# Another order of weight slots at the turn to the second token half, earlier x sums there, and Relu on ScalarE for one more Q pair of each half

## The chip, the cores and the metric

The kernel runs on one core of one Trainium2 chip. The metric is the device time of one execution in microseconds (us), given as the median of several. All executions below were in the fast state, with a mean granted clock between 0.997 and 1.000.

## The reference

A linear attention block and a SwiGLU block read the same normalised input; the second, through a silu, gates the first.

```python
def _A_ref(x, wqkv, wo):                      # 32 heads of 32
    q, k, v = split_heads(x @ wqkv)
    phi = lambda t: jnp.where(t > 0, t + 1, jnp.exp(t)) + 1e-6
    pq, pk = phi(q), phi(k)
    kv = jnp.einsum("bhsd,bhse->bhde", pk, v)
    num, den = pq @ kv, pq @ sum(pk) + 1e-6
    return merge_heads(num / den) @ wo
def _B_ref(x, w_gate, w_up, w_down):
    return (silu(x @ w_gate) * (x @ w_up)) @ w_down
xn = _layernorm(x)                            # x is 1 x 2048 x 1024
return x + _A_ref(xn, ...) * silu(_B_ref(xn, ...))
```

(Shortened: the shapes are 2048 tokens, 1024 columns and 3584 hidden columns.)

## The kernel before

The program works on two token halves, p = 0 and p = 1. In each half it goes through pairs of weight blocks: Q ("q"), gate ("g") and up ("u"), two of the attention output ("s"), and then the down projection. Every product is done with seven block products in place of eight (a Strassen-like scheme), some of them nested twice. So the tensor engine (PE) saves multiplications, and the vector engine (DVE) pays with sums: of weights, of x, and of results in PSUM.

Every operation is recorded first, and a list scheduler inside the kernel then decides the order on each engine. It orders the operations that are ready by a deadline, from which `urgent` is subtracted. What comes out is a fixed program for each engine; at run time each engine takes its instructions strictly in that order and waits on semaphores.

```python
for o in reversed(ops):
    ...
    o.dl = d - o.urgent            # earlier deadline = earlier place
```

Weights are loaded (1 MB) into places that a ring gives out in a fixed order, and their sums are made after the load has landed:

```python
def wload(src, joint, dt=BF16, rd=()):
    s = raw_ring.take()
    dma(list(rd), [s.r], ..., src, dsem("wr%d" % s.k), 1024 * KB)
    c = cmb_ring.take()
    ...
    sums({...}, [cv[:, q] for q in range(4)], [s.r], cr)
```

The evacuation of Q and K applies phi. With `relu`, max(t, 0) comes from ScalarE (ACT) and the last step is a 16-bit sum in SBUF; without, one DVE operation reads PSUM in fp32:

```python
def phi_evac(src, src_r, out_ap, out_r, kind="ps", relu=False):
    ...
    act([src_r], [e.r], ea, src, ACT.Exp, kind)
    dve([e.r], [b.r], lambda h: h.tensor_scalar(ba, ea, 1.0, EPS_PHI, ALU.min, ALU.add), 512, 2.6)
    if not relu:
        dve([src_r, b.r], [out_r], lambda h: h.scalar_tensor_tensor(
            out_ap, src, 0.0, ba, ALU.max, ALU.add), 512)
        return
    r = rl_ring.take()
    act([src_r], [r.r], r.ap(FP16), src, ACT.Relu, kind)
    tt([r.r, b.r], [out_r], out_ap, r.ap(FP16), ba, ALU.add, True)
```

At the turn to the second half, x of that half comes back from memory into the region P, its sums are made, and the slot order for the weights is set:

```python
def turn_pass():
    for q in range(4):
        dma([named("xscr", q)], [P.reg(...)], P.at(...), x_scr[q], dsem("xl%d" % q), 512 * KB)
    combos(XV[1])
    x_inner(XV[1])
    gate[0] = 1
    raw_ring.__init__([(X, 0), (W, 16 * KB), (X, 0)] + [(W, 0), (W, 8 * KB), (W, 16 * KB)] * 5, 8 * KB)
    ...
```

Of the kernel before, what the change touches and what calls it, by code (L numbers as in the profile page):

```python
# [14 lines left out]
KB = 1024  # L15
# [304 lines left out]
def build_kernel(nc, A_x, A_wqkv, A_wo, B_w_gate, B_w_up, B_w_down, out, WINDOW=6, NWARM=15, NPE=2, LEAD=12.0):  # L320
# [12 lines left out]
    with ExitStack() as es:  # L333
# [23 lines left out]
        H = Arena("H", 84 * KB)  # L357
        X = Arena("X", 28 * KB)
        P = Arena("P", 16 * KB)
        W = Arena("W", 52 * KB)  # L360
        TM = Arena("TM", 26 * KB)
# [21 lines left out]
        ps = [es.enter_context(nc.psum_tensor("ps%d" % b, [128, 512], F32)) for b in range(8)]  # L383
# [26 lines left out]
        def sem(name):  # L410
            return es.enter_context(nc.semaphore(name))
# [4 lines left out]
        def dsem(name):  # L416
            if name not in semn:
                semn[name] = sem("d_" + name)
            return semn[name]

        PL = Plan(WINDOW, LEAD)
# [6 lines left out]
        def pe_mm(reads, writes, mms):  # L428
            return PL.op("pe", reads, writes, partial(_mm_group, mms), mm_cost(mms))
# [10 lines left out]
        def act(reads, writes, o, i, func, src="ps", **kw):  # L440
            q = PL.op("act", reads, writes, lambda h: h.activation(o, i, func, **kw),  # L441
                      nel(o) / (1000.0 if "bias" in kw or not isinstance(kw.get("scale", 1.0), float) else 1200.0)
                      + (0.055 if src == "ps" else 0.095))
            if func not in (ACT.Identity, ACT.Relu):
                PL.table(q, func)
            return q

        def dve(reads, writes, fn, n, rate=0.96):
            return PL.op("dve", reads, writes, fn, n / (rate * 1000.0) + 0.07)

        def tt(reads, writes, o, a, b, op, fast=False):
            return dve(reads, writes, lambda h: h.tensor_tensor(o, a, b, op), nel(o), 1.92 if fast else 0.96)  # L452
# [65 lines left out]
        e_ring = Ring(TM, 20 * KB, 1 * KB, 2)  # L518
        q_ring = Ring(TM, 22 * KB, 1 * KB, 2)
        B_ring = Ring(TM, 24 * KB, 1 * KB, 2)  # L520
        rl_ring = Ring(TM, 18 * KB, 1 * KB, 2)
        rr_ring = Ring(TM, 20 * KB, 2 * KB, 1)
        x_ring = Ring(W, 32 * KB, 2 * KB, 4)
        xn_ring = Ring(W, 40 * KB, 2 * KB, 2)
# [30 lines left out]
        def combos(v, after=None):  # L555
            for o, a, b in (("T3", "R11", "R01"), ("T1", "R01", "R00"), ("T2", "R11", "T1"), ("T4", "R10", "T2")):
                for h in range(2):
                    w = {}
                    for nm in (o, a, b):
                        ap, r = v[nm]  # L560
                        n = len(r.keys) // 2
                        w[nm] = ap[:, 2 * h:2 * h + 2, :], Region(r.keys[n * h:n * h + n])
                    q = tt([w[a][1], w[b][1]], [w[o][1]], w[o][0], w[a][0], w[b][0], ALU.subtract, True)
                    if after is not None:
                        q.preds.add(after)
                        after.succs.append(q)
# [142 lines left out]
        def feed(pair):  # L709

            prev = last_pair[0]
            if pair is None or not pair.joint:
                if prev is not None:
                    for w in TAIL:
                        prev.do(w)
                if pair is not None:
                    for w in HEAD:
                        pair.do(w)
            else:
                for w in LINK:  # L720
                    if w[0] == "n":
                        pair.do(w[1:])
                    elif prev is not None:
                        prev.do(w)
            last_pair[0] = pair
# [116 lines left out]
            return ar.at(j * 8 * KB + k * 4 * KB, 4 * KB, FP16).rearrange("p (q t) -> p q t", t=512)[  # L842
                :, :, m * 128:(m + 1) * 128]

        def phi_evac(src, src_r, out_ap, out_r, kind="ps", relu=False):
            e = e_ring.take()
            ea = e.ap(FP16)
            act([src_r], [e.r], ea, src, ACT.Exp, kind)
            b = B_ring.take()
            ba = b.ap(FP16)  # L850
            dve([e.r], [b.r], lambda h: h.tensor_scalar(ba, ea, 1.0, EPS_PHI, ALU.min, ALU.add), 512, 2.6)  # L851
            if not relu:
                dve([src_r, b.r], [out_r], lambda h: h.scalar_tensor_tensor(  # L853
                    out_ap, src, 0.0, ba, ALU.max, ALU.add), 512)
                return
            r = rl_ring.take()
            act([src_r], [r.r], r.ap(FP16), src, ACT.Relu, kind)
            tt([r.r, b.r], [out_r], out_ap, r.ap(FP16), ba, ALU.add, True)

# [12 lines left out]
        def k_evac(i, j, ap, r, kind):  # L872
            if i not in pkv:
                pkv[i] = pk_ring.take()
            s = pkv[i].sub(j * 1024, 1024)
            phi_evac(ap, r, s.ap(), s.r, kind, True)

        def v_dest(i, j):
            return vext[i % 4][:, 4 * j:4 * j + 4, 0:128]
# [67 lines left out]
        for n, (fn, args) in enumerate(((x_load, (0,)), (x_load, (1,)), (wkv_load, (0, 1, 0)), (wkv_load, (0, 1, 1)),  # L947
# [3 lines left out]
            k = len(PL.ops)  # L951
# [6 lines left out]
        for n in range(6):  # L958
            o = pe_mm(wz_r[:1], [bank_r[kvb[2]]], [(ps[kvb[2]][:, 0:128], wz[:, 0:128], wz[:, 0:128], True, True)])
# [74 lines left out]
        for q, kb in enumerate(kvb):  # L1034
            n = 3 if q < 2 else 2
            src = ps[kb][:, 0:129 * n].rearrange("p (g n) -> p g n", n=129)[:, :, 128:129]
# [43 lines left out]
        raw_ring = Places([(W, o * KB) for o in (0, 8, 16)], 8 * KB)  # L1080
# [51 lines left out]
        def xset(stat, w, xv, evac, dring):  # L1132
            def ops(m):
                ws, wr = stat(w, m)
                xa, xr = xv[XOF[m]]
                return 4, [([(ws[q], xa[:, q, :]) for q in range(4)], [wr, xr])]
            return Set(ops, evac, dring)
# [5 lines left out]
        def x_inner(v, xin=xin, places=IN_AT):  # L1143

            for m, at in zip((1, 5), places):
                ap, r = v[XOF[m]]
                B = {(k, j): ap[:, 2 * k:2 * k + 2, 256 * j:256 * j + 256] for k in range(2) for j in range(2)}
                t = [(a.at(o, KB, FP16).rearrange("p (k t) -> p k t", t=256), a.reg(o, KB)) for a, o in at]
                tt([r], [t[1][1]], t[1][0], B[1, 1], B[0, 1], ALU.subtract, True)
                tt([r], [r], B[0, 1], B[0, 1], B[0, 0], ALU.subtract, True)  # L1150
                tt([r], [t[0][1]], t[0][0], B[1, 1], B[0, 1], ALU.subtract, True)
                tt([r, t[0][1]], [t[2][1]], t[2][0], B[1, 0], t[0][0], ALU.subtract, True)
                xin[m] = {1: (B[0, 0], r), 2: (B[1, 0], r), 3: (B[1, 1], r), 5: (B[0, 1], r), 6: t[0], 7: t[1], 4: t[2]}

        def joint_of(jstat, s0, s1, xin=xin):
            def ops(m):
                def f(k):
                    ws, wr = jstat(m, k)
                    xa, xr = xin[m][k]
                    return [(ws[q], xa[:, q, :]) for q in range(2)], [wr, xr]  # L1160
                return f
            return {"1": Joint(ops(1), lambda w, b: (s0, s1)[w].put1(b)),
                    "5": Joint(ops(5), lambda w, b: (s0, s1)[w].put5(b))}
# [20 lines left out]
        def pq_tile(g, j):  # L1184
            o = PQ0 + ((2 * (g // 4) + j) * 4 + g % 4) * KB
            return H.at(o, KB, BF16), H.reg(o, KB)

        def q_pair(p, s, stats, at, go=True):
            stat, jstat = stats

            def evac(w):
                def f(i, j, ap, r, bank):
                    g = 2 * (2 * s + w) + i
                    o, orr = pq_tile(g, j)
                    phi_evac(ap, r, o, orr, "ps" if bank is not None else "sb")
                return f
            s0, s1 = (xset(stat, w, XV[p], evac(w), d_ring) for w in range(2))
            pair = Pair(s0, s1, joint_of(jstat, s0, s1) if QJ[p][s] else None, at)
            if go:
                feed(pair)  # L1200
            return pair
# [489 lines left out]
        def turn_pass():  # L1691

            for q in range(4):
                dma([named("xscr", q)], [P.reg(q * 4 * KB, 4 * KB)], P.at(q * 4 * KB, 4 * KB, FP16), x_scr[q],
                    dsem("xl%d" % q), 512 * KB)
            combos(XV[1])
            x_inner(XV[1])
            gate[0] = 1
            raw_ring.__init__([(X, 0), (W, 16 * KB), (X, 0)] + [(W, 0), (W, 8 * KB), (W, 16 * KB)] * 5, 8 * KB)
            cmb_ring.__init__([(X, 8 * KB), (W, 28 * KB), (X, 8 * KB)] + [(W, 24 * KB), (W, 32 * KB)] * 8, 8 * KB)  # L1700
            in_ring.__init__([(W, 14 * KB), (TM, 8 * KB), (W, 24 * KB), (W, 26 * KB), (W, 42 * KB), (W, 44 * KB)]
                             + [(W, 40 * KB), (TM, 8 * KB), (W, 42 * KB), (W, 44 * KB)] * 8, 2 * KB)
            pump(1)
            last_pair[0] = q_pair(1, 0, got["q", 1, 0], {}, False)
            return last_pair[0]
# [102 lines left out]
```

## Time and profile before

| | before |
|---|---|
| device time, first three executions | 713.54 us (713.01 to 713.55) |
| span of the profile | 711.2 us |
| PE busy | 704.1 us |
| vector engine busy | 634.0 us |
| ScalarE busy | 416.6 us |
| HBM traffic | 127 GB/s over the span |

PE is busy 99% of the span, so what can be won is the time in which it stands still. That time is best measured from the start of one matmul to the start of the next: here 0.216 us for 512 columns and 0.109 us for 256. What is over that I call "lost". The prediction below shows the lines and the three places in the middle of the program where time is lost: near 130, 408 and 431 us.

### The profile page before, as it was taken

What the parts mean: (1) busy time and instruction counts of PE and PEld (TensorE: products, weight loads), DVE (VectorE), ACT (ScalarE), POOL (GpSimd) and SP (SyncE); (2) the same over time, 40 slices, a digit from 0 to 9 for tenths busy, and PEclk for the clock granted to TensorE, in tenths of its full rate; (3) what the DMA queues carried; (4) which work ended last, traced back from release to release, by engine and by line L of the source; (5) the groups of instructions that cost most, each with busy time, mean ns of one, the idle gap of its engine ahead of it and who ended that gap; (6) DMA issues with size and microseconds to landing.
All of it is one profiled execution on the core that took longest, in us unless ns stands there. A gap on an engine that the chain in (4) does not pass through costs nothing.

```text
span 711.2 us, 11395 instructions
## 1 busy us (share of the span) xinstructions
PE 704.1 (99%) x4170; PEld 388.4 (55%) x4181; DVE 634.0 (89%) x1533; ACT 416.6 (59%) x809; POOL 14.1 (2%) x35
## 2 busy tenths in 40 slices
PE   9999999999999999999999999999999999999997
PEld 4444445555555555555555455555555555565654
DVE  7999858999999999988966999999999999798863
ACT  4788755888679566664212156776886756531212
POOL 2111000000000000000000000000000000000000
PEclk9999999999999999999999999999999999999999
DMA  9654134345664252326485954132816241656663
GB/s 295 149 119 90 30 118 126 112 140 187 182 180 145 93 171 94 119 66 175 139 190 172 254 160 149 60 119 94 207 60 189 79 149 60 178 141 162 142 156 96
DMA packets 140870, 98.64 MB, mean 139 GB/s; under 512 B 34960, under 2 KB 137872, under 8 KB 140816
## 3 DMA queue, kind: packets, MB, share of 16 engines
q1 hardware_dynamic: 140528, 97.74, 49.3%
q8 instruction: 32, 0.52, 0.3%
q10 hardware_dynamic: 288, 0.20, 0.1%
q14 instruction: 22, 0.18, 0.1%
HBM read 77.59 MB, written 12.71 MB: 127 GB/s over the span
## 4 chain that ended last, share of the span: by engine, by line
PE 92%; DVE 5%; DMA 2%; issue 1%; ACT 0%; SPq 0%
PE ps L309 92%; DMA X<-in_A_wqkv_dram 1%; DVE TM L452 1%; DVE ps L452 1%; DVE W L452 1%; DVE H L853 1%; DVE X L452 0%; DMA W<-in_A_x_dram 0%; ACT TM L441 0%; DVE H L1043 0%; DVE TM L851 0%; PE ps L316 0%; DVE P L452 0%; DVE stats L773 0%; SPq L455 0%
## 5 line engine op out<-in xcount | busy, mean ns | idle before, releaser
L309 PE MATMUL ps<-X,W 128*128 128x512 f16 (+2 forms) x1372 | 288.8, 350 | 0.4 <-DVE ps L452 0.4
L441 ACT ACTIVATE TM<-ps 128x512 f16<-128x512 f32 (+3 forms) x380 | 199.6, 552 | 100.9 <-PE ps L309 97.6
L309 PE MATMUL ps<-H,W 128*128 128x512 f16 (+2 forms) x1090 | 217.9, 350 | 0.4
L452 DVE TENSOR_TENSOR W<-W 128x1024 f16<-128x1024 bf16 (+5 forms) x416 | 185.8, 479 | 5.3 <-PE ps L309 4.5
L309 PEld LDWEIGHTS ps<-X,W 128*128 128x128 f16 (+1 forms) x1372 | 132.3, 98 | 104.1 <-DVE ps L452 1.2
L309 PEld LDWEIGHTS ps<-H,W 128*128 128x128 f16 (+1 forms) x1096 | 106.1, 98 | 94.8 <-DVE ps L452 0.6
L452 DVE TENSOR_TENSOR ps<-ps,TM 128x256 f32<-128x256 f32 (+1 forms) x250 | 131.3, 527 | 13.6 <-PE ps L309 10.8
L441 ACT ACTIVATE ps<-ps 128x512 f32<-128x512 f32 (+1 forms) x174 | 85.6, 492 | 94.5 <-PE ps L309 94.0
L309 PE MATMUL ps<-P,W 128*128 128x256 f16 (+1 forms) x516 | 99.7, 319 | 0.0
L441 ACT ACTIVATE H<-ps 128x512 f16<-128x512 f32 (+1 forms) x126 | 74.7, 604 | 39.4 <-PE ps L309 39.4
L452 DVE TENSOR_TENSOR H<-H 128x1024 f16<-128x1024 f16 (+5 forms) x126 | 71.2, 578 | 0.5 <-ACT H L441 0.4
L441 ACT ACTIVATE TM<-TM 128x512 f16<-128x512 f32 (+1 forms) x68 | 42.3, 627 | 48.4 <-DVE TM L452 47.0
L309 PEld LDWEIGHTS ps<-P,W 128*128 128x128 f16 (+1 forms) x516 | 50.3, 98 | 29.0 <-ACT TM L441 0.4
L309 PE MATMUL ps<-W 128*128 128x256 f16 (+1 forms) x330 | 62.0, 282 | 1.0 <-DVE ps L452 1.0
L452 DVE TENSOR_TENSOR TM<-ps,TM 128x512 f32<-128x512 f32 (+3 forms) x63 | 41.5, 659 | 12.6 <-PE ps L309 12.1
L452 DVE TENSOR_TENSOR H<-H,TM 128x512 f16<-128x512 f16 x112 | 44.9, 416 | 7.1 <-ACT H L441 7.0
L309 PEld LDWEIGHTS ps<-W 128*128 128x128 f16 (+1 forms) x330 | 31.3, 98 | 32.9 <-DVE ps L452 2.7
L452 DVE TENSOR_TENSOR TM<-TM 128x512 bf16<-128x512 f16 (+2 forms) x73 | 29.4, 411 | 6.5 <-ACT TM L441 3.9
L309 PE MATMUL ps<-H,X 128*128 128x512 bf16 (+1 forms) x147 | 34.6, 379 | 0.2
L309 PE MATMUL ps<-H,P 128*128 128x512 bf16 (+1 forms) x108 | 26.4, 379 | 0.1
L452 DVE TENSOR_TENSOR H<-ps,TM 128x512 f16<-128x512 f32 (+1 forms) x35 | 24.0, 686 | 2.3 <-PE ps L309 1.5
L309 PEld LDWEIGHTS ps<-H,X 128*128 128x128 f16 (+1 forms) x150 | 14.3, 98 | 17.0 <-DMA H<-in_A_wqkv_dram 0.6
(95 smaller groups left out, 400.2 us busy)
## 6 DMA issues: line engine op xcount, KB each, us to landing
W<-in_B_w_gate_dram SPq DMA_DIRECT2D x14, 1024.0 KB, 5.4
W<-in_B_w_up_dram SPq DMA_DIRECT2D x13, 1024.0 KB, 5.6
W<-in_B_w_down_dram SPq DMA_DIRECT2D x14, 896.0 KB, 6.1
H<-in_A_wqkv_dram SPq DMA_DIRECT2D x8, 512.0 KB, 8.2
H<-r_scratch SPq DMA_DIRECT2D x32, 128.0 KB, 3.8
W<-m_scratch SPq DMA_DIRECT2D x4, 1024.0 KB, 5.4
s_scratch<-TM SPq DMA_DIRECT2D x32, 128.0 KB, 2.0
TM<-in_A_x_dram SPq DMA_DIRECT2D x16, 256.0 KB, 3.7
```

The source lines that it names most:

```text
L309: last = h.matmul(o, l, r, start=st, stop=sp, skip_group_check=True)
L441: q = PL.op("act", reads, writes, lambda h: h.activation(o, i, func, **kw), nel(o) / (1000.0 if "bias" in kw or not isinstance(kw.get("sca ...
L452: return dve(reads, writes, lambda h: h.tensor_tensor(o, a, b, op), nel(o), 1.92 if fast else 0.96)
L853: dve([src_r, b.r], [out_r], lambda h: h.scalar_tensor_tensor(out_ap, src, 0.0, ba, ALU.max, ALU.add), 512)
```

## The change

The intent is to take the vector engine off PE's path at those places. The first up weights of half 2 go to a free place (W 0) and not to X 0, where the first Q weights still lie (W, X and P are regions of the on-chip memory, and W 0 is the first place in W); the x sums of half 2 get an earlier deadline; and two more Q pairs let ScalarE do the Relu.

```diff
-        rl_ring = Ring(TM, 18 * KB, 1 * KB, 2)
+        rl_rings = Ring(TM, 18 * KB, 1 * KB, 2), Ring(H, 40 * KB, 1 * KB, 2)
...
-            if not relu:
+            if relu is None:
...
-            r = rl_ring.take()
+            r = relu.take()
...
-            phi_evac(ap, r, s.ap(), s.r, kind, True)
+            phi_evac(ap, r, s.ap(), s.r, kind, rl_rings[0])
...
-                    phi_evac(ap, r, o, orr, "ps" if bank is not None else "sb")
+                    phi_evac(ap, r, o, orr, "ps" if bank is not None else "sb", rl_rings[p] if s == p else None)
...
+            k = len(PL.ops)
             combos(XV[1])
             x_inner(XV[1])
+            for o in PL.ops[k:]:
+                o.urgent = 6.0
...
-            raw_ring.__init__([(X, 0), (W, 16 * KB), (X, 0)] + [(W, 0), (W, 8 * KB), (W, 16 * KB)] * 5, 8 * KB)
+            raw_ring.__init__([(X, 0), (W, 16 * KB), (W, 0), (X, 0), (W, 8 * KB), (W, 16 * KB)] + [(W, 0), (W, 8 * KB), (W, 16 * KB)] * 5, 8 * KB)
```

More of the change, by code (lines that the diff above doesn't have):

```diff
@@ L843, in xt_half, with phi_evac @@
                 :, :, m * 128:(m + 1) * 128]
-        def phi_evac(src, src_r, out_ap, out_r, kind="ps", relu=False):
+        def phi_evac(src, src_r, out_ap, out_r, kind="ps", relu=None):
             e = e_ring.take()
```

## The prediction

> **What bounds the kernel now.** I read the page's first part first, then the slices. Columns of the first line: busy time, share of the span, number of instructions. In the slices, one digit is 17.8 us.
>
> ```profile
> PE 704.1 (99%) x4170; PEld 388.4 (55%) x4181; DVE 634.0 (89%) x1533; ACT 416.6 (59%) x809; POOL 14.1 (2%) x35
> ...
> PE   9999999999999999999999999999999999999997
> ...
> DVE  7999858999999999988966999999999999798863
> ACT  4788755888679566664212156776886756531212
> PEclk9999999999999999999999999999999999999999
> ```
>
> The tensor engine is busy in every slice at full clock, and the vector engine is full in most of them. The change alters no matmul (4180 in both built programs, same shapes), so all it can win is the time in which PE stands still. That is at most 711.2 - 704.1 = 7.1 us of the span, and much of it is the start and the end, which the change does not touch. So I looked for PE's gaps one by one, in its instructions in order of time (columns: start, duration, engine, line, operation, count; in brackets the idle time before it and what ended it).
>
> ```profile
> 128.72 1.25 PE L309 MATMUL ps<-X,W 128*128 128x256 f16 x6
> 130.26 0.39 PE L309 MATMUL ps<-W 128*128 128x256 f16 x2 [0.30 <-DVE ps L452]
> ...
> 406.35 1.03 PE L309 MATMUL ps<-W 128*128 128x512 f16 x4
> 408.06 0.39 PE L309 MATMUL ps<-W 128*128 128x256 f16 x2 [0.68 <-DVE ps L452]
> ...
> 429.71 1.03 PE L309 MATMUL ps<-X,W 128*128 128x512 f16 x4
> 431.09 1.04 PE L309 MATMUL ps<-X,W 128*128 128x512 f16 x4 [0.35 <-DVE ps L452]
> ```
>
> The three gaps after the opening that name a releaser all end with a vector add from PSUM to PSUM. The bracket understates them: the end of a matmul is modelled and includes a tail. From start to start, a 512-column matmul takes 0.216 us here and a 256-column one 0.109, so the losses are 408.06 - 406.35 - 4 x 0.216 = **0.84 us**, 431.09 - 429.71 - 0.864 = **0.52 us**, and, with the last matmul before 130.26 a 512-column one that the merged row hides, **0.47 us**. One of 0.05 us follows at 435. Together 1.88 us. The other start-to-start losses after the opening are 0.02 to 0.2 us each, beside an M build, a reciprocal or the end of the gate/up phase, except 0.74 us at the very end. None of those is touched.
>
> Why the vector engine was late shows in the chain of waits in order of time (start, duration, what):
>
> ```profile
> 384.09 8.59 DMA X<-in_A_wqkv_dram
> 392.68 0.02 issue
> 392.70 0.69 DVE X L452
> ...
> 407.66 0.35 DVE ps L452
> 408.01 0.05 issue
> 408.06 16.64 PE ps L309 x96
> ```
>
> The load of the first Q weights of token half 2 takes 8.6 us, and from its landing the vector engine works through a backlog until it comes to the add that PE needs. The table of stretches confirms it (length, then busy time of PE, PEld, DVE, ACT, POOL; then clock, DMA share, GB/s):
>
> ```profile
> 117.00:131.80 14.80, 14.50 (x91) 7.93 (x88) 14.72 (x44) 9.84 (x19) 0.00 (x0) 1.00 0.54 161
> 375.00:394.00 19.00, 19.00 (x107) 10.26 (x105) 12.75 (x26) 3.95 (x7) 0.00 (x0) 1.00 0.68 212
> 394.00:408.00 14.00, 13.38 (x66) 6.26 (x64) 14.00 (x37) 3.11 (x6) 0.00 (x0) 1.00 0.99 220
> 408.00:432.00 24.00, 23.59 (x133) 12.89 (x134) 23.74 (x56) 14.92 (x27) 0.00 (x0) 1.00 0.63 180
> ```
>
> Before 394 the vector engine has 19.00 - 12.75 = 6.25 us to spare; after it, none.
>
> **What the Trainium skill says.** (1) "Perfetto Trace Analysis", per-engine timelines: a matmul's reported end is estimated. The trace agrees: 0.38 us is reported for matmuls that follow each other every 0.216, so I used starts. (2) "VectorE: DVE Perf Modes", perf-mode tier table: a two-tensor operation with a PSUM operand runs at 1x, a 16-bit one in SBUF at 2x. The trace agrees: the phi sum at L853 (fp32 in) has 0.60 us from start to start, the fp16 512-column sum 0.33. (3) "ScalarE: Activation LUTs": Relu is filler in every table set, so no table load is added (section on table sets), though its rules for kernel authors send Relu to VectorE. The built programs have equally many table loads. The existing K-side phi already runs Relu beside Exp in this kernel. That rule need not hold where VectorE is the full engine. (4) "DMA: Bandwidth & Descriptors", anatomy of one DMA: the issuing sequencer waits, not the DMA engines. The trace agrees: transfers leave the sync queue strictly in its program order, so an early-placed transfer that waits holds up those behind it.
>
> **The change part by part.**
>
> *x sums of half 2 sooner.* They are 8 operations of 1024 columns (0.60 us from start to start) and 8 of 512 (0.33 us): 8 x 0.60 + 8 x 0.33 = 7.4 us of vector work. In the kernel before, 4 + 2 of the first kind and all of the second stand between 394 and 408, 6 x 0.60 + 8 x 0.33 = 6.2 us of those 14. In the built changed program most of them stand before the adds of the down projection's joint step, that is before 394, in time that is nearly half idle. Even if 5 us move, the add wanted at 407.2 comes several us sooner: the 0.84 us goes. Three of the four loads that feed them (512 KB each, issued at 383.5, 384.6 and 386.5 beside the Q weights) now stand some ten places earlier in the sync queue, near 370 to 375, when PE has just read the region for the last time (P, at 374 to 375). I therefore also expect the Q load to shrink from 8.6 us to about the 5.4 us that 1 MB loads take as a median on this page. It can't be issued sooner (its place X is read until about 382).
>
> *Slot order.* The first up weights go to W 0 instead of X 0; the Q weights after them go to X 0. X 0 comes free only when the first Q pair is done, so the up load was issued at 427.1 and landed after 5.5 us at 432.6, for matmuls at 433.7, with its sums in between: just in time. W 0 is last read by the fourth product of the down projection, which ends at 414.3; the load can leave then, 13 us sooner. The sums can be spread over 414 to 433 instead of crowding into 432 to 436. This, with the 5 us of backlog gone, should take most of the 0.52 and the 0.05. No instruction is added.
>
> *Relu on ScalarE*, for the first Q pair of half 1 (117 to 132) and the second of half 2 (452 to 466). Each has 8 evacuations; each trades one 0.60 us vector operation for one of 0.33 and one ScalarE operation of 0.52 (back to back). Vector: 16 x 0.27 = 4.3 us less. ScalarE: 16 x 0.52 = 8.3 us more. In half 1 the vector engine is full (14.72 of 14.80), so 2.2 us less there should take the 0.47 us at 130; but ScalarE goes from 9.84 to 9.84 + 8 x 0.52 = 14.0 of 14.8 us, close to full itself. I count 0.35 of 0.47. In half 2 the pair lies where PE loses nothing (32.00 us busy of 32.00 between 440 and 472), so I count 0.
>
> Sum: 0.80 + 0.40 + 0.05 + 0.35 = 1.6 us won. The whole schedule around both places is reordered by the kernel's own list scheduler (598 changed lines on the vector engine), with no slack on PE, so I take off 0.3 us for new small waits: **1.3 us won, 713.54 - 1.3 = 712.2 us.**
>
> **The rivals.**
> - *ScalarE becomes the bound in the first Q pair.* For it: 14.0 of 14.8 us. The table switch to Silu at 131.8 (1.28 us) must wait for the last Exp, so the first gate evacuations and their banks come late. Against it: the K/V phase already runs ScalarE at 18.03 of 20.00 us with PE unhurt, and Relu frees the PSUM bank without waiting for the vector engine. It would cost the 0.47 us gain and up to 1 us more: 713 to 714.
> - *The early x loads or sums stand in the way.* The sync queue and the vector engine are in order; a sum whose load is late blocks the joint adds near 380 to 390, which PE needs, and a load that waits for PE blocks the transposes behind it. For it: these adds now stand behind x sums. Against it: the DMA share is 0.23 to 0.40 between 378 and 382, so 512 KB should land well within 6 us. It would move the 0.84 us to an earlier place: about 713.0.
> - *The stalls move.* The vector engine is full from 394 to about 480 before; with 5 us less backlog there, later work is only pulled forward, but a new order can make single adds late. If half of the gain is given back: 712.7.
> - *Everything works and nothing is given back*: 713.54 - 1.88 = 711.7.
>
> **Range and chances.** The floor is the last rival less 0.3 us of run-to-run spread (the three runs span 0.54 us): 711.4. The ceiling takes a net gain near zero: 713.5. Two per cent is 14.3 us, twice PE's whole idle time, so faster by 2% is ruled out nearly; a loss of 14 us would need a blocked queue that I don't see. I give 0.01 and 0.01.
>
> **What would show it.** Right: the waits of PE at 130, 408 and 431 are gone or below 0.1 us each; the vector engine works through x sums before 394 and has fewer than 3 us idle between 375 and 394; the Q load takes under 7 us; the up load is issued near 415; the table shows vector busy about 4.3 us lower and ScalarE 8 us higher, of which the half-2 part moves nothing. Wrong: PE's idle time stays above 6.5 us of the span with gaps at new places that name ScalarE or a DMA, or matmul starts between 375 and 395 show gaps where there were none.

## The result

The changed kernel took 712.56 us (median of 6, 711.96 to 713.21) against 713.27 us (median of 6, 712.41 to 713.72) for the kernel before. The ratio is 0.9991 with a 95% interval of 0.9979 to 1.0004. All ratios here are taken by program from the fast runs of both kernels in the same rounds, so they are not quite the ratio of the medians. By time alone, this is the same. What the change did has to be read from the traces.

The page of the changed kernel starts with this line (busy time, share of the span, instructions); its span is 710.5 us:

```profile
PE 705.0 (99%) x4181; PEld 388.5 (55%) x4181; DVE 631.4 (89%) x1533; ACT 423.3 (60%) x825; POOL 14.1 (2%) x35
```

PE now stands still for 710.5 - 705.0 = 5.5 us. (The eleven more matmuls are records that were missing in the other trace; the programs have equally many, and both traces show 4181 weight loads. Each missing record left a gap of 0.05 us, so about 0.5 us of the 7.1 us before was not idle time at all; a_again below, with the same records missing, shows 7.0 us. The starts are the safer measure.) The vector engine has 2.6 us less and ScalarE 6.7 us more. PE's instructions in order of time show what became of the three waits (start, duration, engine, line, operation, count):

```profile
127.65 0.39 PE L309 MATMUL ps<-W 128*128 128x256 f16 x2
...
131.34 0.38 PE L309 MATMUL ps<-W 128*128 128x256 f16 x2
...
407.12 1.25 PE L309 MATMUL ps<-W 128*128 128x512 f16 x6
408.21 0.38 PE L309 MATMUL ps<-P,W 128*128 128x256 f16 x2
...
429.63 1.03 PE L309 MATMUL ps<-X,W 128*128 128x512 f16 x4
430.59 0.61 PE L309 MATMUL ps<-P,W 128*128 128x256 f16 x4
```

No bracket with idle time is left at any of these places. By the starts, 0.06 us is lost at 127.65 and nothing at 131.34, where 0.47 was lost before; at 408 nothing (six matmuls, four of 512 columns and two of 256, follow without a break: 4 x 0.216 + 2 x 0.109 = 1.08 and 408.21 - 407.12 = 1.09); and 430.59 - 429.63 - 0.864 = 0.09 us at 430. Gone too is a wait that the prediction overlooked: in the kernel before, the matmul at 434.01 started 0.11 us late, behind a weight load (PEld) that waited for a sum of the late up weights:

```profile
434.01 0.76 PEld L309 LDWEIGHTS ps<-P,W 128*128 128x128 f16 x6 [0.22 <-DVE W L452]
```

The table of stretches for the same windows (length, then busy time of PE, PEld, DVE, ACT, POOL; clock, DMA share, GB/s):

```profile
117.00:131.80 14.80, 14.80 (x96) 8.43 (x95) 14.31 (x49) 11.61 (x24) 0.00 (x0) 1.00 0.50 166
375.00:394.00 19.00, 19.00 (x111) 10.62 (x110) 17.06 (x38) 4.71 (x9) 0.00 (x0) 1.00 0.82 215
394.00:408.00 14.00, 14.00 (x71) 6.72 (x70) 13.19 (x33) 3.00 (x6) 0.00 (x0) 1.00 0.79 225
408.00:432.00 24.00, 24.00 (x138) 13.32 (x137) 22.97 (x57) 15.58 (x29) 0.00 (x0) 1.00 0.65 160
```

The vector engine does 4.3 us more work before 394 and is no longer full after it. So far it goes as intended: the turn wins 0.84 + 0.52 + 0.11 + 0.05 - 0.09 = 1.43 us, the first Q pair 0.35 us net of two losses that grew (0.02 at 136 and 0.04 at 141). But the chain of waits in order of time has something new in it (start, duration, what):

```profile
179.51 9.60 DMA W<-in_B_w_up_dram
...
191.32 0.05 issue
191.37 158.82 PE ps L309 x938
```

PE lost 0.46 us near 191. The weight loads there wait for adds into PSUM, which stand in the vector queue behind the first sums of up weights, and these sums waited for a load that took 9.6 us:

```profile
189.14 1.30 DVE L452 TENSOR_TENSOR W<-W 128x256 f16<-128x256 bf16 x4 [0.70 <-DMA W<-in_B_w_up_dram]
```

In the kernel before, the same load took 8.8 us, and nothing was lost. The opening, too, ended later: PE's unbroken run of real matmuls began at 10.84 us against 10.16. The two programs are the same in both places, so the question was whether these losses belong to the change.

### The profile page after: what moved, and what is told of

It reads as the page before. It is cut to its first block, busy times and chain, and to the rows that moved or that the text cites. A ratio compares the mean times of both kernels' runs of the same rounds, so it can differ in the third digit from the quotient of the medians.

```text
span 710.5 us, 11436 instructions
## 1 busy us (share of the span) xinstructions
PE 705.0 (99%) x4181; PEld 388.5 (55%) x4181; DVE 631.4 (89%) x1533; ACT 423.3 (60%) x825; POOL 14.1 (2%) x35
## 4 chain that ended last, share of the span: by engine, by line
PE 96%; DMA 2%; SPq 0%; DVE 0%; issue 0%; ACT 0%
PE ps L309 96%; DMA W<-in_B_w_up_dram 1%; DMA H<-in_A_wqkv_dram 1%; SPq L455 0%; DVE W L452 0%; PE ps L316 0%; DVE ps L452 0%; DVE TM L452 0%; SPq L757 0%; ACT TM L441 0%
## 5 line engine op out<-in xcount | busy, mean ns | idle before, releaser
L441 ACT ACTIVATE TM<-ps 128x512 f16<-128x512 f32 (+3 forms) x386 | 202.6, 555 | 101.9 <-PE ps L309 99.0
L452 DVE TENSOR_TENSOR W<-W 128x1024 f16<-128x1024 bf16 (+5 forms) x412 | 183.1, 478 | 3.5 <-PE ps L309 2.1
L441 ACT ACTIVATE H<-ps 128x512 f16<-128x512 f32 (+1 forms) x132 | 78.4, 606 | 38.3 <-PE ps L309 38.3
L452 DVE TENSOR_TENSOR H<-H,TM 128x512 f16<-128x512 f16 (+1 forms) x120 | 48.0, 417 | 8.5 <-ACT H L441 8.3
L452 DVE TENSOR_TENSOR TM<-TM,W 128x512 f16<-128x512 f16 (+1 forms) x39 | 14.0, 363 | 11.5 <-ACT TM L441 11.4
```

Source lines behind the costliest of these rows:

```text
L441: q = PL.op("act", reads, writes, lambda h: h.activation(o, i, func, **kw), nel(o) / (1000.0 if "bias" in kw or not isinstance(kw.get("sca ...
L452: return dve(reads, writes, lambda h: h.tensor_tensor(o, a, b, op), nel(o), 1.92 if fast else 0.96)
```

## The experiments

Each trace was read in the same way. The table gives the median time, the ratio to the kernel before in the same rounds, and, from the one profile of each, the lost time at four places, the landing times of two loads, and PE's **steady stretch**: from the first real matmul after the opening to the end of the last one. The stretch leaves out the opening and the last stores, which vary by themselves.

| kernel | median us | ratio (95% interval) | lost at 130 | at 191 | at 408 | at 430 to 436 | up load at 179 | Q load at 384 | steady stretch |
|---|---|---|---|---|---|---|---|---|---|
| before, first profile | 713.54 | | 0.47 | 0 | 0.84 | 0.67 | 8.8 | 8.6 | 698.03 |
| b_again (before) | 713.20 | 1.0002 (0.9987 to 1.0017) | 0.46 | 0 | 0.38 | 0.67 | 8.3 | 8.1 | 697.92 |
| changed, first profile | 712.56 | 0.9991 (0.9979 to 1.0004) | 0.06 | 0.46 | 0 | 0.09 | 9.6 | 5.5 | 696.72 |
| a_again (changed) | 712.77 | 0.9988 (0.9973 to 1.0003) | 0.07 | 0.13 | 0 | 0.09 | 9.3 | 5.7 | 696.41 |
| relu_half1 | 713.61 | 1.0005 (0.9989 to 1.0022) | 0.07 | 0.26 | 1.03 | 0.68 | 9.4 | 8.8 | 698.15 |
| relu_half2 | 713.91 | 1.0013 (0.9997 to 1.0029) | 0.46 | 0.23 | 0 | 0.67 | 9.3 | 7.5 | 697.35 |
| turn_only | 712.07 | 0.9986 (0.9968 to 1.0003) | 0.47 | 0 | 0 | 0.09 | 9.1 | 5.9 | 696.55 |
| slots_only | 711.68 | 0.9983 (0.9968 to 0.9998) | 0.46 | 0 | 0 | 0 | 8.5 | 7.2 | 696.87 |
| sums_only | 714.38 | 1.0017 (1.0000 to 1.0033) | 0.47 | 0 | 1.24 | 1.12 | 8.9 | 9.3 | 698.87 |
| q_sum_moved | 714.66 | 1.0025 (1.0011 to 1.0039) | 0.47 | 0.40 | 1.01 | 0.68 | 9.5 | 7.6 | 698.56 |
| x_later | 711.37 | 0.9973 (0.9958 to 0.9987) | 0.07 | 0 | 0 | 0.09 | 5.9 | 6.4 | 696.30 |
| x_later_b | 711.39 | 0.9980 (0.9967 to 0.9992) | 0.06 | 0 | 0 | 0.09 | 5.5 | 5.7 | 696.24 |
| turn_x_later | 711.61 | 0.9980 (0.9967 to 0.9994) | 0.47 | 0 | 0 | 0.09 | 5.2 | 5.6 | 696.56 |
| slots_relu1_x_later | 711.76 | 0.9983 (0.9970 to 0.9995) | 0.06 | 0 | 0 | 0 | 5.5 | 7.3 | 696.23 |

(The stretches of slots_only and b_again contain 0.44 and 0.41 us lost near 26 us, where PE waits for sums of weights of the opening; no other run shows this.)

My theory at the start was that the wins at the three places are real, and that the losses at 191 and in the opening are chance landings of loads. The first rival was that the wait at 191 comes from the change. The second was that the win at the turn does not split as I had said.

### The changed kernel once more

No edit.

> The changed kernel once more, unedited. Theory: the wait of 0.46 us at 191 us and 0.5 us more in the first 11 us of its first profile are the landing times of loads that vary from run to run (the program is the same there as in the kernel before), so in a new profile the waits at 130, 408 and 431 are gone again (each below 0.12 us), and the one at 191 differs or is absent; timed ratio 0.9978 to 0.9990 to the kernel before. Rival: the wait at 191 is made by the change; then it is there again with 0.4 to 0.5 us and the ratio stays near 0.9991.

The three wins are there again to within 0.03 us, and the wait at 191 is 0.13 us where it was 0.46. It varies with the landing, so the larger wait was not a fixed part of the change. The opening was late again (10.88 us).

### Relu in half 1 alone

```diff
 (the changed kernel, with the old slot order and urgent = 0.0)
-rl_rings[p] if s == p else None
+rl_rings[p] if s == p == 0 else None
```

> The kernel before with Relu on ScalarE for the first Q pair of half 1 alone. Theory: the wait at 130 falls from 0.47 us to about 0.06, the waits at 408 (0.84), 431 (0.52) and 435 stay; 0.3 to 0.4 us won. Rival (ScalarE becomes the bound there): a new wait behind ScalarE between 130 and 137 of over 0.2 us. If the waits at the turn change as well, the parts are not independent.

The wait at 130 went from 0.47 to 0.07, and the places at the turn stayed, as expected. No wait behind ScalarE appeared: at 136, after the table load, 0.11 us is lost where 0.09 was. The time did not show it (ratio 1.0005): the interval is 2.4 us wide (0.0033 of 713), for 0.35 us in question, and in this kernel's profile 0.26 us at 191 and a longer wait at 408 (1.03 us) stood against it. The wait at 408 was not to change. That it did was the first sign that 0.84 was one draw of something that varies.

### Slot order and sums without any Relu

```diff
 (the changed kernel)
-rl_rings[p] if s == p else None
+None
```

> Slot order and earlier x sums, no Relu edit. Theory: the waits at 408, 431 and 435 go (under 0.1 us in sum left), the one at 130 stays at 0.47; about 1.3 us won. Rival (vector relief of the Relu edit of half 2 is needed too): 0.2 us or more is left between 400 and 440.

As expected: 0.47 us at 130 is back, the turn has 0.09 left. The Relu edit of half 2 is not needed for the turn.

### The new slot order alone

```diff
 (the changed kernel, no Relu edit)
-                o.urgent = 6.0
+                o.urgent = 0.0
```

> The kernel before with the new slot order alone. Theory (the prediction's split): the wait at 408 stays (0.7 to 1.0 us), since the up load plays no part before 414; the waits at 431 and 435 (0.52 and 0.05) go for the most part, since the up load leaves at 414 and its sums are spread. Rival (431 is backlog of the x sums): 431 stays at 0.4 us or more.

This is a miss. With the slot order alone nothing is lost at the turn, at 408 neither, though the load that it moves is issued only at 414. What it shares with 408 is the schedule: with another slot order the list scheduler laid the whole turn out anew. PE's line at the place, and the place of the first sum of the late Q weights (X<-X) on the vector engine (two views of slots_only):

```profile
407.01 1.24 PE L309 MATMUL ps<-W 128*128 128x512 f16 x6
408.09 0.38 PE L309 MATMUL ps<-P,W 128*128 128x256 f16 x2
```

```profile
391.40 0.69 DVE L452 TENSOR_TENSOR ps<-ps,TM 128x512 f32<-128x512 f32 x1
...
393.14 0.61 DVE L452 TENSOR_TENSOR W<-W 128x896 f16<-128x896 bf16 x1
393.68 0.68 DVE L452 TENSOR_TENSOR X<-X 128x1024 f16<-128x1024 bf16 x1
```

The Q load was issued at 384.66 and landed after 7.2 us at 391.9. Its first sum now stands at 393.7, behind other work, and so waits for nothing. For 408 this profile is no clean test, though. In the old order that sum comes 1.14 us after the add from PSUM to PSUM shown here (390.99 and 392.13 in relu_half2 below), so at about 392.5 here, and this load had landed by then: the old order would have waited for nothing either. The same reckoning holds for every profile with the new order. Their Q loads took 5.5 to 7.3 us (eight profiles), those with the old order 7.5 to 9.3 us (six), and the new order also changed the order of the transfers at the turn. So nothing is lost at 408 because the load lands sooner, or because its sum stands later; these runs do not part the two. At 431 to 435 it is shown: every program with the old slot order loses 0.67 us or more there, and every one with the new order at most 0.09.

### The earlier x sums alone

```diff
 (the changed kernel, no Relu edit, old slot order)
-            raw_ring.__init__([(X, 0), (W, 16 * KB), (W, 0), (X, 0), (W, 8 * KB), (W, 16 * KB)] + ...
+            raw_ring.__init__([(X, 0), (W, 16 * KB), (X, 0)] + ...
```

> The kernel before with the earlier x sums alone. Theory: the wait at 408 goes (under 0.1 us); 431 falls from 0.52 but does not vanish, 0.1 to 0.4 us, and the late up load (landing near 432) leaves 0.05 to 0.3 us at 433 to 436. Rival (everything at the turn is backlog of the x sums): nothing over 0.1 us is left between 400 and 440, and the slot order adds nothing.

The second miss, and the worse one: 1.24 us is lost at 408 and 1.12 at 435, 2.4 us where the four profiles with the turn of the kernel before lose 0.7 to 1.7. In time it is the slower one too (ratio 1.0017, with an interval that begins at 1.0000). The vector engine in order of time, then PE (in brackets the idle time before it and what ended it):

```profile
393.73 0.70 DVE L452 TENSOR_TENSOR ps<-ps,TM 128x512 f32<-128x512 f32 x1
396.51 0.43 DVE L452 TENSOR_TENSOR TM<-TM 128x512 bf16<-128x512 f16 x1 [2.09 <-DMA TM<-TM]
```

```profile
408.59 0.39 PE L309 MATMUL ps<-W 128*128 128x256 f16 x2 [1.08 <-DVE ps L452]
...
433.76 0.38 PE L309 MATMUL ps<-P,X 128*128 128x256 f16 x2
435.05 1.25 PE L309 MATMUL ps<-P,W 128*128 128x256 f16 x6 [0.90 <-DVE W L452]
```

The x sums were done early, as asked, but the vector engine then stood for 2.09 us before an addition whose operand was still being transposed by a DMA (issued at 392.95, landed 3.5 us later). In this schedule that addition had come too early in the queue. The wait at 435 comes from sums of the up weights, which the vector queue reached only at 434.7, for matmuls due at 434.0; their load, issued at 427.69, had landed by 433.0, so at the end it was the queue that was late and not the load. With the new slot order this wait is gone, and in this profile the earlier sums mend nothing by themselves. Nor did they shorten the Q load: it took 9.3 us here, though three of the four x loads had left before 376.

### Relu in half 2 alone

```diff
 (the changed kernel, with the old slot order and urgent = 0.0)
-rl_rings[p] if s == p else None
+rl_rings[p] if s == p == 1 else None
```

> The kernel before with Relu on ScalarE for the second Q pair of half 2 alone. Theory: no wait of PE changes (130, 408, 431, 435 all as before; none between 440 and 480 but the 0.09 beside the reciprocal), time the same within 0.3 us, vector engine about 2.1 us less busy and ScalarE 4 to 5 us more. Rival (it helps the turn through the order): the waits at 408 or 431 fall.

Between 440 and 480 PE's waits did not change, as expected: there was nothing to win. But the wait at 408 was 0 in this profile, with the turn's program as in the kernel before. So the same program loses 0.84, 0.38 or nothing there. The next run is the third of these.

### The kernel before once more

No edit.

> The kernel before, unedited, as one more profile of it. Theory: waits at 130, 408, 431 as in its first profile within 0.2 us; the landing of the up weights' load issued near 179 us is 8.8 to 9.6 us and any wait near 191 follows from it alone (none up to about 9.1, then about as much as it is later); the first steady matmul of the opening starts anywhere between 10.1 and 10.9 us. Rival (these two belong to the change): 8.8 us, no wait near 191 and 10.2 us again.

The waits at 130 and 431 are as in the first profile to within 0.01 us; the one at 408 is 0.38. The first sum of the late Q weights on the vector engine explains it. Here it is in three profiles whose programs are the same at this place: the kernel before, b_again, and relu_half2 (there with the add ahead of it).

```profile
392.70 0.69 DVE L452 TENSOR_TENSOR X<-X 128x1024 f16<-128x1024 bf16 x1 [0.91 <-DMA X<-in_A_wqkv_dram]
```

```profile
392.56 0.69 DVE L452 TENSOR_TENSOR X<-X 128x1024 f16<-128x1024 bf16 x1 [0.45 <-DMA X<-in_A_wqkv_dram]
```

```profile
390.99 0.70 DVE L452 TENSOR_TENSOR ps<-ps,TM 128x512 f32<-128x512 f32 x1 [0.22 <-PE ps L309]
...
392.13 0.68 DVE L452 TENSOR_TENSOR X<-X 128x1024 f16<-128x1024 bf16 x1
```

The idle time before that sum was 0.91, 0.45 and 0 us, and in relu_half1 1.09. PE lost 0.84, 0.38, 0 and 1.03 us fifteen microseconds later. The vector engine is full from 394 to 408, so in this program the time in which it stands before that sum comes out at PE, less 0.07 us of slack. The Q load took 8.6, 8.1, 7.5 and 8.8 us in these four: that is what varies.

For the wait at 191, relu_half2 and q_sum_moved have the program of the kernel before up to 370 us, and they lost 0.23 and 0.40 us there. Their up loads took 9.3 and 9.5 us. Over the ten profiles with the stores in their old place, loads of 8.3 to 9.1 us lost nothing, and loads of 9.3 to 9.6 us lost 0.13 to 0.46. So the wait at 191 is not made by the change. In this profile, the kernel before was at 10.13 us at the end of the opening; over all fourteen profiles it was between 10.13 and 11.15, with unchanged and changed kernels at both ends.

### The first Q sum moved down in the vector queue

The direct test of that reading: in the kernel before, after scheduling, the first sum of the late Q weights and the two small ones that follow from it are put five vector operations later. Nothing else moves.

```diff
 (the kernel before; shortened)
+        at = PL.order.index(qsum[0])          # the first sum of q_load(1, 0)
+        moved, passed, end = [qsum[0]], 0, at
+        while passed < 5:
+            end += 1
+            o = PL.order[end]
+            if any(p in o.preds for p in moved):
+                moved.append(o)
+            elif o.eng == "dve":
+                passed += 1
+        PL.order[at:end + 1] = [o for o in PL.order[at:end + 1] if o not in moved] + moved
```

> The kernel before with one move after scheduling: on the vector engine, the first sum of the late Q weights and the two small ones that follow from it stand five operations (about 2.9 us) later. New theory: the wait at 408 is the time by which the Q load lands behind the place of its first sum in the vector queue, passed on one to one through 14 us of full vector work (0.91, 0.45, 1.09 and 0 us of idle before that sum gave 0.84, 0.38, 1.03 and 0 us at PE); then the idle time and the wait at 408 are both gone (under 0.1 us) while 431 stays at 0.52 and nothing else changes; 0.4 to 0.9 us won. Rival (my prediction: the backlog of x sums makes the add late): the same work stands ahead of the add, so the wait stays at 0.4 us or more. Possible spoiler: the x loads themselves land late, then a wait for them takes the place.

The spoiler came true. The wait for the Q load is gone, but the operations that moved up are x sums, and now these wait for their own load. The vector engine, then PE:

```profile
394.62 0.69 DVE L452 TENSOR_TENSOR X<-P 128x1024 f16<-128x1024 f16 x1 [0.83 <-DMA P<-x_scratch]
```

```profile
409.57 0.39 PE L309 MATMUL ps<-W 128*128 128x256 f16 x2 [0.85 <-DVE ps L452]
```

PE lost 1.01 us after 0.83 of idle time. So the test did not show the wait going away, and it was slower (1.0025); in its profile, 0.40 us at 191 and a late end of the opening (11.15 us), which the move did not make, add to that. It agrees with the wider form of the theory, that any load reached too early by the full vector queue costs PE about the same time. It does not exclude that the order of the work had a part too: the loss is 0.18 us over the idle time, and I did not settle where that comes from. The rival from my prediction, that the sheer amount of x sums ahead of the add makes it late, is half right: it is why the queue is full and hands every wait on.

### The stores of x behind the up load

The up load at 179 stands between two 512 KB stores of x to memory, the last of four. They can go later.

```diff
 (the changed kernel)
-                if (p, k, n) == (0, "g", 1):
-                    for q in range(4):
+                if (p, k, n) in ((0, "g", 1), (0, "u", 1)):
+                    for q in ((0, 1) if k == "g" else (2, 3)):
```

> The changed kernel with the last two of four stores of x to memory placed behind the up weights' load at 179 us, not on both sides of it. Theory: that load then lands in 5.5 to 7 us instead of 8.8 to 9.6, so no wait near 191 is left in any run; 0 to 0.5 us faster than the changed kernel, which would be the fastest. Rival (stores don't slow the load): it still takes over 8.5 us.

> The changed kernel with the x stores behind the up load, once more beside the two below. Theory: no wait near 191 (up load about 6 us), body as in its first profile, ratio 0.997 to 0.998. Rival (its first result was a lucky chip state): 0.999.

Both runs agree. The load landed after 5.9 and 5.5 us (this view's columns: what, queue, kind, count, size, time to landing), the wait at 191 was gone, and the medians were 711.37 and 711.39 us. This is from the list of transfers of x_later:

```profile
W<-in_B_w_up_dram SPq DMA_DIRECT2D x1, 1024.0 KB, 5.9
```

Beside the changed kernel on the same chip (711.19 to 712.00 against 712.01 to 712.96) it is faster, by 1.4 us in the medians, where the traces show 0.1 to 0.5 us at 191. The rest is not explained. In the two executions that were profiled (711.22 and 712.01 us) the difference is 0.79 us, of which 0.68 is the opening and 0.11 the steady stretch.

> The same without any Relu edit. Theory: only the wait at 130 comes back (0.47 against 0.07 and about 0.05 of small ones), 0.3 to 0.4 us slower than x_later_b. Rival (ScalarE work costs as much as it saves): equal.

> Slot order, Relu in half 1 alone and the x stores behind the up load; no earlier x sums, no Relu in half 2. Theory after slots_only: nothing over 0.1 us is lost between 400 and 440, so it equals x_later_b within 0.2 us; the early sums and the Relu of half 2 are worth nothing on average. Rival: without the early sums the Q load lands after the place of its first sum in some runs, and 0.1 to 0.5 us is lost at 408.

The last two are x_later less the Relu edits, and x_later less the early sums and the Relu of half 2. In the traces turn_x_later has 0.47 us at 130 again and a stretch that is 0.32 us longer than x_later_b's; that agrees with 0.35. slots_relu1_x_later has the same stretch as x_later_b (696.23 and 696.24 us), so in these profiles the earlier sums and the second Relu win nothing on PE. In time the three (711.39, 711.61, 711.76) cannot be told apart; their ranges overlap. I name x_later as the best, as it was measured twice: 0.2 to 0.3% faster than the kernel before, with intervals that leave out 1.

## Why the prediction was right, and where it was not

**The total.** 712.2 was predicted and 712.56 measured, inside the range, with 0.98 of the chances on "within 2%". That alone says little: 0.7 us was won in the medians (713.27 to 712.56) where 1.3 was forecast, the interval of the ratio includes 1, and the 713.27 us of the kernel before lie inside the range too. The steady stretch, which leaves out the opening, is 1.31 us shorter in the one pair of first profiles. What bounds the kernel was read rightly: PE's own idle time is the most that could be won.

**The terms of the sum.** The trace of the changed kernel gives 1.43 us at the turn, where 0.80 + 0.40 + 0.05 = 1.25 was set down (the 0.11 us at 434 was missing from the list of losses, so that 1.88 us should have been 1.99), and 0.35 us at the first Q pair, where 0.35 was. The signs named in advance held as well: the Q load took 5.5 us (under 7), the up load left at 414.45 (near 415), and the vector engine was idle for 1.94 us between 375 and 394 (under 3). For the Q load the number held, but not the reason: the early x loads alone (sums_only) left it at 9.3 us, and it is shorter wherever the new slot order is in.

**The step that failed** is the split of the turn: "Even if 5 us move, the add wanted at 407.2 comes several us sooner: the 0.84 us goes", laid to the x sums, and the slot order, with that backlog gone, "should take most of the 0.52 and the 0.05". By experiment the slot order alone takes all that is lost from 431 on, and in its profile nothing is lost at 408 either; the x sums alone take none of it, and their profile loses 0.7 to 1.7 us more than the four with the turn of the kernel before. The two edits are not two terms. Each makes the list scheduler lay out the turn anew, and what decides at 408, as far as these runs show, is whether a load, or a transposed tile, has landed when the vector engine's fixed queue comes to it. The two edits together do give room: with them the first Q sum stands at 398.1, 8.7 us behind the landing, and with the slot order alone 1.8 us behind. In the runs here that room bought nothing. Q loads of up to 9.3 us were seen, so it might in others; that stays open.

**What was mis-sized.** The 0.84 us was taken as a fixed loss. The four profiles with that program lost 0.84, 0.38, 1.03 and 0 us, so 0.56 us on average. The gain to be expected at the turn was then 0.56 + 0.67 - 0.09 = 1.14 us and not 1.43; that the first profile happened to show 0.84 is luck.

**The deduction of 0.3 us for new small waits.** The new schedule made 0.09 at 430, 0.06 at 127 and 0.06 at 136 and 141 together, and nothing else over 0.02. The new wait at 191 was not made by it. So the deduction was about the right size, for the changed kernel alone; what hid the rest in the time was the spread of landings in the opening and at 191.

**The rivals.** ScalarE did not become the bound: in half 1 it was busy 11.61 of 14.80 us, and not the 14.0 that were feared, and its table load came at 133.55 instead of 131.83, later by more than the 0.7 us by which the whole trace was later, and PE lost 0.02 us more there (at 136) than before. That early work stands in the way of others was told as a rival, and it is what sums_only showed, near 396 and not near 385; in the changed kernel as a whole it did not come true.

**Vector and ScalarE busy time** moved by -2.6 and +6.7 us and not by -4.3 and +8.3. The signs are right. The sizes were worked out from one start to the next, while the page's busy time includes the tails of operations that nothing follows at once. I take that as the reason; it was not tested.

## What to carry to other kernels

Where one engine is full for many microseconds, a wait in its in-order queue can come out almost whole at the bound engine at the end of the full stretch, as it did in four profiles here, so look for the first idle time before the stretch and for the load that ended it, not at the wait's own place. Take two profiles of the same kernel before a gap of a microsecond is booked as a gain: one that hangs on a landing time is a spread and not a number. And with a scheduler between the edit and the program, test each part of a change alone; its effect can come through the new layout rather than through what the edit was made for.

## What the Trainium skill lacked or had wrong

- "DMA: Bandwidth & Descriptors", anatomy of one DMA, gives a fit of 2.0 us plus bytes over 436 GB/s (measured there on another issue path); for 1 MB that is 4.4 us, as an estimate from the page. The runs here show 5.2 to 5.9 us for the up load with the stores behind it, and 8.3 to 9.6 us with a 512 KB store on each side. The page has nothing on how much the landing of one load spreads from run to run: 7.5 to 8.8 us for the same Q load in the same program.
- "ScalarE: Activation LUTs", rules for kernel authors, sends relu to VectorE. With VectorE full, eight Relus on ScalarE took a wait of PE from 0.47 to 0.06 us, and PE lost 0.06 us more at two later places, with ScalarE busy 11.61 of 14.80 us. That table lacks the condition that VectorE has room; the skill has it elsewhere ("Perfetto Trace Analysis", optimizing Scalar/DVE operations: with a saturated DVE, moving work to ScalarE may make sense).
- "Perfetto Trace Analysis", per-engine timelines, says that a matmul's end is estimated, but not by how much. Here a 512-column matmul is shown with 0.38 us and the next one starts after 0.216, so waits of up to 0.16 us do not show as idle time at all, and all others are shown 0.16 us too short (0.68 for 0.84, 0.35 for 0.52).
- No page has a measure of how an in-order wait passes through a full engine. Here it came out almost whole: 0.91, 0.45 and 1.09 us of idle time on the vector engine came out as 0.84, 0.38 and 1.03 us at PE, fifteen microseconds later.
